# Two fused kernels on one core: one written-out sequence of 1011 operations exchanged for another

## The chip, the cores and the metric

The kernel runs on one core of a Trainium2 chip. The metric is the device time of one execution in microseconds; the value used is the median of several runs. A core has five engines that run side by side, each working through its own instructions strictly in order: TensorE (PE in the profile, its weight loads PEld), VectorE (DVE), ScalarE (ACT), GpSimd (POOL) and SyncE (SP), which here only issues transfers. GpSimd issues transfers too, those that add into their target.

## The reference

The first half is an attention without softmax. With a = S1 x and b = S2 x (8 values each), phi(x) is the outer product of a and b (64 values). The output of this half becomes the input x of a second half that mixes tokens.

```python
q_p, k_p = (phi(q), phi(k))                       # (4, 4, 1088, 64)
kv = np.einsum('bhsf,bhsd->bhfd', k_p, v)
z = np.sum(k_p, axis=2)
num = np.einsum('bhsf,bhfd->bhsd', q_p, kv)
den = np.einsum('bhsf,bhf->bhs', q_p, z)[..., None] + 1e-06
x = num / den                                     # then laid out as (4, 1088, 128)
...
theta = x @ w_theta
zr, zi = x * np.cos(theta), x * np.sin(theta)
y = einsum('ts,bsd->btd', w_tok_r, zr) + einsum('ts,bsd->btd', w_tok_i, zi)
u = x + y
out = u + np.maximum(u @ w_ch, 0.0)
```

There are 4 batches, 4 heads, 1088 tokens and 128 channels. The denominator is small against its terms, so the kernel computes it in several exact slices (the "levels").

## The kernel before

**Operations and sequence.** The kernel does not issue instructions while it walks its loops. Each piece of work is first recorded as an operation (`L.op`, line 133) with an engine, a planned duration, a function that issues its instructions, and the buffers that it writes and reads. 1011 operations are recorded, numbered in the order of recording. The text `ORDER` (line 29) names these numbers in the sequence in which they are issued. `lay` (line 207) walks that sequence once with the planned durations; its start times decide two things alone: which slot of a buffer class each buffer gets (line 229), and how many filler matmuls `issue` (line 273) puts ahead of an operation for which the plan has TensorE wait (line 279). A filler is a 128x384 bf16 matmul on zeros (`spin`, line 434, L435 in the profile); 11 stand at the very start (line 438), 16 more are operations of their own (the "fill" stage, line 440), and one is a marker (line 1432). Because every engine runs in order, the place of a number in `ORDER` fixes what each instruction stands behind on its engine, and on SP and POOL which transfer is issued behind which.

**Stages, as far as the steps below need them.** Names in quotes are those of the tiles in the profile.

- The first transfers (SP): the keys of batch 0 (`load`, line 674), the small matrices S1 and S2 ("st", lines 454 and 455), the two square weights ("zs" from w_sq, `weight` line 646), then keys, queries and values of the other batches and the 17 row blocks of the token-mixing weights (w_tok, 1088 KB each). The weights come as 64-bit floats and are rebuilt as 32-bit floats by ACT (L647, L649) and DVE (L388, L384).
- Key sums (`key_sums`, line 683): ACT squares a batch's keys (L699), a matmul with ones adds them up ("ps<-sm,ones"), DVE derives a rounding step (L388 "sm<-sm") and rounds the keys ("hf<-big,sm"), then takes the remainder ("big<-big,hf"). TensorE sums products of the rounded keys ("ps<-hf", 36 narrow matmuls) and of the remainders ("ps<-big,big" and "ps<-big", the rest sums).
- Key features (`kfeatures`, line 769): TensorE transposes keys (L792), ACT copies them out (L795), TensorE applies S1 and S2 ("ps<-sbk,g"), DVE forms the outer products ("g<-sm,ps"), TensorE multiplies with the values ("ps<-g,big" 128x64).
- `chain` (line 838) and `levels` (line 1050) make the exact denominator: short DVE and TensorE steps, then nine groups of four matmuls for each batch ("ps<-mv,hf" and "ps<-mf,big", 128x96), ACT's copy (L1068), and a chain of DVE steps on "lv".
- `outputs_x` (line 1129): numerators (transposes L1155, "ps<-g,sm"; for batches 2 and 3 `small_numerators`, line 1100, with DVE transposes L1112 and one block of 64 narrow matmuls "ps<-zs,g"), then theta, sine and cosine on ACT (L1197 to L1203). `balance` (line 1218) squares two batches' x on ACT (L1222) and puts a common scale on them, which the third batch's phases wait for.
- Token mixing: "ps<-big,zs" with 128x384 and 128x320 for batches 0 and 1 (`mix_row`, line 1247), and for batches 2 and 3 together a Strassen-Winograd product (`winograd`, line 1299) with half-sized blocks (288 and 256 wide).
- `finish` (line 1273) and `finish_by_tokens` (line 1289): last weight, ReLU and sum on DVE (L391), transpose on DVE (L1279), and the store by SP: four transfers for each block (L1283), one for each of the two last blocks (L1297).

**Matmuls and instructions.** A transpose or a bf16 or f16 matmul is one weight load and one matmul in the trace; another f32 matmul of the program is two such pairs. The program's 1253 matmuls are 2066 in the trace, with as many weight loads.

Of the kernel before, what the change touches and what calls it, by code (L numbers as in the profile page):

```python
# [26 lines left out]
TINY = 2.0**-60  # L27
UP = 256.0
ORDER = """
    0 1 35 12 5 13 10 11 107 14 53 15 16 18 54 108 57 55 101 19 58 20 47 48 59 17 3 4 60 61 62 63 64 65 66 38 67  # L30
    68 21 138 142 125 50 144 36 102 79 95 69 49 70 71 56 72 40 73 74 22 80 81 309 96 311 147 23 51 75 24 126 145
    7 250 257 261 28 127 82 39 97 128 129 251 98 25 8 99 103 310 143 312 104 105 139 76 77 78 140 31 263 192 193
    146 41 307 308 166 84 119 120 32 85 33 37 131 266 313 109 86 148 149 267 132 150 151 110 111 167 168 314 186
    100 344 268 269 152 153 87 88 205 209 345 106 112 154 244 9 347 113 133 187 42 188 134 26 264 89 2 245 34 90
    91 189 43 285 135 198 199 194 195 141 92 93 155 238 156 157 270 271 272 273 158 274 159 160 161 262 162 163
    6 211 164 165 286 287 121 239 29 122 27 114 190 315 123 346 171 348 200 201 94 364 424 116 428 425 426 429
    432 214 233 427 215 216 359 202 430 44 360 169 431 433 434 435 234 235 288 236 252 316 206 333 172 436 117
    366 327 124 437 438 196 45 253 173 207 210 439 328 217 118 174 175 440 317 339 83 441 442 365 325 170 176
    326 443 318 319 320 321 191 130 136 115 444 334 177 331 265 178 445 323 197 453 52 137 240 324 246 446 341
    241 332 30 213 247 179 203 204 180 335 336 454 460 449 322 46 340 450 447 218 219 242 220 221 222 258 275  # L40
    276 342 277 278 279 448 456 455 457 349 394 451 248 458 212 452 280 350 343 351 259 181 467 281 535 536 469
    531 470 537 532 463 459 533 282 283 534 527 528 529 538 461 530 539 223 224 225 226 227 228 254 464 476 183
    540 182 462 229 230 231 468 471 465 352 473 541 472 474 466 184 284 542 232 475 477 478 543 353 354 544 355
    243 545 546 547 548 484 249 255 256 549 356 384 483 492 493 485 185 386 361 479 480 556 481 260 486 494 385
    552 553 550 551 357 559 560 557 558 554 563 561 555 571 562 208 564 565 482 358 362 367 487 374 566 567 578
    570 572 489 289 573 574 575 576 363 488 368 329 579 369 495 290 568 580 569 581 370 371 496 497 375 291 577
    292 582 586 490 641 642 643 491 588 377 583 293 589 372 376 584 618 619 595 585 294 620 295 296 297 644 645
    379 646 380 381 621 590 622 596 623 373 419 330 396 395 592 591 298 498 668 669 670 303 382 421 383 671 672
    673 674 675 378 664 665 420 397 237 300 404 387 666 587 593 409 422 597 388 598 647 648 649 650 411 624 594
    423 406 305 410 405 389 667 398 412 676 599 600 601 602 299 301 391 407 413 408 390 603 604 499 392 393 399  # L50
    400 401 500 414 306 836 402 403 415 677 651 652 678 501 502 416 679 417 503 504 505 506 302 680 418 507 681
    508 515 682 683 840 509 337 684 685 688 690 338 686 687 730 726 727 731 732 728 521 729 865 722 723 724 653
    304 835 654 510 869 733 605 625 839 626 627 628 629 691 725 834 689 692 693 734 735 736 694 695 737 696 655
    630 631 738 739 740 741 742 743 632 698 746 748 697 699 744 747 700 656 701 511 512 705 657 707 703 749 658
    708 709 702 711 745 606 633 713 750 751 704 752 753 516 814 815 715 706 795 796 797 816 710 714 607 513 712
    817 798 755 804 837 754 756 716 717 777 779 780 863 719 799 781 818 819 718 522 868 768 770 800 759 761 720
    771 772 805 762 820 757 782 763 806 774 838 867 841 773 807 808 809 810 811 758 721 760 634 767 769 514 764
    801 893 608 864 765 635 766 831 776 775 778 783 784 832 861 802 851 852 821 853 854 833 891 862 523 524 855
    856 822 857 803 860 880 858 785 525 926 889 881 882 890 859 907 894 866 883 884 885 659 892 636 886 786 929
    930 870 823 827 787 788 789 790 609 895 928 791 792 793 610 908 887 896 794 871 872 873 909 910 932 911 912  # L60
    874 875 876 877 517 518 913 914 888 915 828 931 842 965 933 916 934 843 844 845 927 878 879 948 846 847 949
    950 920 939 848 849 850 812 935 937 813 637 897 638 639 936 526 611 612 613 951 940 924 952 953 954 898 899
    900 901 902 964 938 941 942 943 944 829 640 955 903 956 519 824 520 825 826 977 987 988 925 660 945 946 947
    661 830 662 663 960 904 905 966 989 614 906 615 967 968 969 616 961 617 921 917 918 919 970 971 972 973 957
    974 922 923 975 990 962 978 979 991 958 959 976 997 998 992 980 993 999 994 995 963 1000 996 981 982 983 984
    985 986 1006 1008 1007 1009 1001 1002 1010 1003 1004 1005
"""
WARM = 0
FILL = 5.0
# [36 lines left out]
class Layout:  # L106
# [26 lines left out]
    def op(self, eng, dur, fn, w=(), r=(), hold=(), lk=0, fly=0.0, chan=0.0):  # L133
        o = Op()
        o.lk, o.fly, o.stage, o.chan = lk, fly, self.stage, chan
        o.i, o.eng, o.dur, o.fn = len(self.ops), eng, dur, fn
        pred = set()
        o.bufs = []

        def parts(x):  # L140
            return x if isinstance(x, tuple) else (x, None)

        def hits(table, b, key):
            t = table.get(b, {})
            return [v for k, v in t.items() if k is None or key is None or k == key]

        for x in r:
            b, key = parts(x)
            pred.update(hits(self.last_w, b, key))
            o.bufs.append(b)  # L150
        for x in w:
            b, key = parts(x)
            pred.update(hits(self.last_w, b, key))
            for s in hits(self.readers, b, key):
                pred.update(s)
            o.bufs.append(b)
        for x in r:
            b, key = parts(x)
            self.readers.setdefault(b, {}).setdefault(key, set()).add(o.i)
        for x in w:  # L160
            b, key = parts(x)
            if key is None:
                self.last_w[b] = {None: o.i}
                self.readers[b] = {}
            else:
                self.last_w.setdefault(b, {})[key] = o.i
                self.readers.setdefault(b, {})[key] = set()
        o.bufs = list(dict.fromkeys(o.bufs + list(hold)))
        for b in o.bufs:
            b.ops.append(o.i)  # L170
        pred.discard(o.i)
        o.pred = sorted(pred)
        self.ops.append(o)
        return o
# [145 lines left out]
def kernel(  # L320
# [13 lines left out]
    S, DM = out.shape[1], out.shape[2]  # L334
# [35 lines left out]
    op, buf = L.op, L.buf  # L370
# [78 lines left out]
    sp = fixed((2, NS), F32, "sp")  # L449
# [7 lines left out]
    if wide:  # L457
        st = fixed((NS,), I64, "st")
        y = fixed((NS,), I32, "sy")
        z = fixed((NS,), I32, "sz")  # L460
        op("V", 0.1, lambda: V.memset(st().bitcast(F32), 0.0), [st], [])
        op("S", 0.25, read_small, [st], [], lk=3)

        def words():
            w = st().bitcast(I32).rearrange("p (n t) -> p n t", t=2)
            return w[:, :, 0], w[:, :, 1]

        op("A", 0.25, lambda: A.activation(sp()[:, 0], words()[1].bitcast(F32), AF.Prelu, scale=2.0**-112,
                                           alpha=-(2.0**32)), [(sp, 0)], [st])

        def unpack():
            wl = words()[0]
            x = sp()[:, 0].bitcast(I32)
            ts(x, x, 3, ALU.logical_shift_left)
            stt(x, wl, 29, x, ALU.logical_shift_right, ALU.bitwise_or)
            ts(y(), x, -(1 << 23), ALU.bitwise_and)
            ts(z(), wl, 0x1FFFFFFF, ALU.bitwise_and)

        op("V", 0.85, unpack, [(sp, 0), y, z], [st], lk=2)
        op("A", 0.25, lambda: A.activation(sp()[:, 1], z(), AF.Copy, scale=2.0**-52), [(sp, 1)], [z])  # L480
        vop(NS, lambda: tt(V, sp()[:, 1], sp()[:, 1], y().bitcast(F32), ALU.mult), [(sp, 1)], [y])
    else:
        op("V", 0.2, lambda: V.memset(sp(), 0.0), [sp], [])
        op("S", 0.25, read_small, [(sp, 0)], [], lk=3)

    def powers(mfn, m, n, name):

# [1013 lines left out]
```

## Time and profile before

| what | value |
|---|---|
| median of 3 runs | 222.49 us (221.52 to 222.84) |
| the profiled execution | 222.86 us |
| its span, first to last instruction | 221.1 us, so 1.76 us lie around it |
| PE busy | 212.8 us (96%), 2066 matmuls |
| DVE, ACT, POOL busy | 167.0, 114.9, 45.5 us |
| filler matmuls | 39 |
| bytes moved by transfers | 40.19 MB |

A busy PE means that at least one matmul is in flight; matmuls overlap, so how long one holds the engine is read from the distance between two starts, not from its duration. In a line of the timeline the brackets at its end say how long the engine was idle before and what ended that; "issue" means that nothing the profile shows held the instruction back. A row of the stretches view gives, for each engine, its busy time in that stretch and, behind an x, the number of its instructions.

### The profile page before, as it was taken

To read this page: it belongs to the slowest core of one execution; us is meant where nothing else is said; L and a number is where in the kernel's file an instruction comes from. 1 tells how busy PE (TensorE), PEld (TensorE's weight loads), DVE (VectorE), ACT (ScalarE), POOL (GpSimd) and SP (SyncE) were. 2 spreads that over 40 slices of the span, in tenths; PEclk is the share of its full clock that TensorE was granted. 3 is DMA by queue.
4 is the path that set the end of the run, shared out by engine and by line. 5 is a ranking of instruction groups with operands and counts; after the bars stand their busy time and mean duration, and the time that the engine had idled before them with its cause. 6 is when DMAs were issued, how large, how long until landed. Compare 5 with 4: busy or idle time off the path is not lost.

```text
span 221.1 us, 5129 instructions
## 1 busy us (share of the span) xinstructions
PE 212.8 (96%) x2066; PEld 160.8 (73%) x2066; DVE 167.0 (76%) x360; ACT 114.9 (52%) x237; POOL 45.5 (21%) x81
## 2 busy tenths in 40 slices
PE   7999998999999999999999999999999999999993
PEld 3786987777776757686666685778888787788772
DVE  2899897999899999899999969953899005324951
ACT  3988657989699798949740042377930000000000
POOL 1168260101200000100040083000273165030000
PEclk9999999999999999999999999999999999999999
DMA  6999999985509008948862069411098489772673
GB/s 183 411 424 319 394 418 362 418 270 211 205 9 369 30 0 268 373 170 260 345 115 41 0 104 178 73 20 20 0 185 139 80 149 180 122 111 34 100 115 69
DMA packets 26987, 40.19 MB, mean 182 GB/s; under 512 B 18260, under 2 KB 19284, under 8 KB 24788
## 3 DMA queue, kind: packets, MB, share of 16 engines
q1 hardware_dynamic: 22212, 30.30, 40.0%
q0 software_dynamic: 4752, 9.57, 24.4%
q8 instruction: 16, 0.26, 0.4%
q14 instruction: 7, 0.06, 0.1%
HBM read 28.07 MB, written 2.23 MB: 137 GB/s over the span
## 4 chain that ended last, share of the span: by engine, by line
PE 80%; DVE 5%; ACT 5%; SPq 3%; DMA 3%; issue 2%
PE ps L404 73%; SPq L1283 3%; DMA big<-k_l 2%; PE ps L1188 2%; PE ps L1155 2%; PE ps L792 2%; ACT big L649 2%; PE ps L435 1%; DVE lv L384 1%; DVE g L384 1%; DMA out<-g 1%; PE ps L1035 1%; ACT big L699 1%; DVE big L391 1%; ACT big L1003 1%
## 5 line engine op out<-in xcount | busy, mean ns | idle before, releaser
L404 PE MATMUL ps<-big,zs 128*128 128x384 f32 (+4 forms) x366 | 102.8, 426 | 0.4 <-DVE big L384 0.4
L404 PEld LDWEIGHTS ps<-big,zs 128*128 128x128 f32 x366 | 65.6, 190 | 27.6 <-DVE big L384 1.6
L1267 ACT COPY g<-ps 128x384 f32<-128x384 f32 (+1 forms) x6 | 2.6, 464 | 44.6 <-DVE g L1279 32.0
L384 DVE CUSTOM_DVE_ANT_0 big<-big,big 128x2176 uint16<-128x2176 uint16 x17 | 21.5, 1285 | 0.3
L647 ACT ACTIVATE big<-zs 128x1088 f32<-128x1088 f32 x17 | 20.6, 1215 | 2.3 <-DMA zs<-w_tok 1.8
L649 ACT ACTIVATE big<-zs 128x1088 int32<-128x1088 uint32 (+1 forms) x18 | 20.8, 1167 | 1.1 <-DVE big L384 1.1
L404 PE MATMUL ps<-mf,big 128*128 128x96 f32 x72 | 14.6, 296 | 0.9 <-issue 0.9
L384 DVE TENSOR_TENSOR zs<-ps,g 128x768 f32<-128x768 f32 (+2 forms) x20 | 12.3, 629 | 3.6 <-ACT g L1201 2.2
L391 DVE SCALAR_TENSOR_TENSOR big<-ps,even,big 128x256 f32<-128x256 f32 (+1 forms) x10 | 4.8, 493 | 12.6 <-PE ps L404 12.6
L404 PE MATMUL ps<-big,big 128*32 128x32 f32 (+2 forms) x320 | 14.1, 220 | 0.2 <-issue 0.2
L1328 POOL DMA_DIRECT2D big<-zs x8 | 7.0, 1132 | 34.7 <-PE ps L404 29.4
L1328 POOL DMA_DIRECT2D big<-big x8 | 9.2, 1638 | 19.7 <-issue 19.7
L404 PEld LDWEIGHTS ps<-big,big 128*32 128x32 f32 (+1 forms) x320 | 10.3, 118 | 3.4 <-issue 1.5
L398 POOL DMA_DIRECT2D g<-big x6 | 7.8, 1433 | 23.4 <-ACT g L1267 23.4
L1295 ACT COPY g<-ps 128x128 f32<-128x128 f32 x2 | 0.5, 265 | 23.0 <-PE ps L1293 22.0
L388 DVE TENSOR_SCALAR big<-big 128x1088 int32<-128x1088 int32 x17 | 12.1, 719 | 0.0
L404 PEld LDWEIGHTS <-hf 128*32 128x32 bf16 (+1 forms) x252 | 10.8, 99 | 1.7 <-issue 0.5
L435 PE MATMUL ps<-idle 128*128 128x384 bf16 x39 | 10.6, 398 | 1.3 <-POOL idle L437 1.3
L404 PEld LDWEIGHTS ps<-mf,big 128*128 128x128 f32 x72 | 10.9, 191 | 1.1 <-issue 1.1
L384 DVE TENSOR_TENSOR g<-lv 128x768 f32<-128x768 f32 x12 | 11.1, 953 | 0.3
L404 PE MATMUL ps<-w,big 128*128 128x128 f32 x76 | 10.9, 280 | 0.4 <-ACT g L1295 0.4
L404 PEld LDWEIGHTS ps<-w,big 128*128 128x128 f32 x76 | 9.9, 192 | 1.5 <-ACT g L1295 0.6
(199 smaller groups left out, 399.6 us busy)
## 6 DMA issues: line engine op xcount, KB each, us to landing
zs<-w_tok SPq DMA_DIRECT2D x17, 1088.0 KB, 5.6
big<-k_l SPq DMA_DIRECT2D x7, 576.0 KB, 8.1
big<-q_l SPq DMA_DIRECT2D x4, 576.0 KB, 15.6
big<-v_l SPq DMA_DIRECT2D x4, 576.0 KB, 8.0
big<-big POOLq DMA_DIRECT2D x8, 272.0 KB, 6.1
big<-zs POOLq DMA_DIRECT2D x8, 272.0 KB, 3.9
zs<-big POOLq DMA_DIRECT2D x8, 272.0 KB, 5.7
big<-hf POOLq DMA_DIRECT2D x3, 576.0 KB, 9.9
```

The lines of the kernel that those rows point to most:

```text
L384: eng.tensor_tensor(out=o, in0=a, in1=b, op=f)
L388: (eng or V).tensor_scalar(out=o, in0=a, scalar1=s1, scalar2=s2, op0=op0, **kw)
L391: (eng or V).scalar_tensor_tensor(out=o, in0=a, scalar=s, in1=b, op0=op0, op1=op1)
L398: op("G", 1.05, lambda: G.dma_start(dst(), src(), accum_op=ALU.add), w, r, chan=chan)
L404: T.matmul(o, lhs, rhs, start=start, stop=stop, skip_group_check=True)
L435: T.matmul(nowhere(), idle()[:, 0:P], idle(), start=True, stop=True, skip_group_check=True)
L647: op("A", 0.22 + n * 0.0009, lambda: A.activation(dfn(), words_of(raw(), n)[1].bitcast(F32), AF.Prelu, scale=2.0**-112, alpha=-(2.0**32)), ...
L649: op("A", 0.22 + n * 0.0009, lambda: A.activation(stp(), words_of(raw(), n)[0].bitcast(U32), AF.Copy, scale=2.0**-29), [stp], [raw])
L792: T.transpose(tr()[:, i * P:(i + 1) * P], kx()[:, g * GC + i].rearrange("p h d -> p (h d)"), ident())
L1155: T.transpose(tr()[:, i * P:(i + 1) * P], qp()[:, i * H + 2 * n:i * H + 2 * n + 2].rearrange("p h i j -> p (h i j)"), ident())
L1283: SY.dma_start(out[b, t0 - o:t0 + w, f * SQ:(f + 1) * SQ].rearrange("(c j) i -> j c i", j=SQ), ot()[f * SQ:(f + 1) * SQ, :o + w].rearrange ...
L1328: op("G", 1.05, lambda i=i: G.dma_start(dst[0](i), x[0](i), accum_op=ALU.add), [dst[1](i)], [x[1](i)], chan=ADD_FLY3)
```

## The change

The text `ORDER` is replaced by another sequence of the same 1011 numbers. The planned duration of the transfer of S1 and S2 goes from 0.25 to 0.9 (this is a number of the plan; it changes no instruction). Slots and fillers follow from the new walk.

```diff
 ORDER = """
-    0 1 35 12 5 13 10 11 107 14 53 15 16 18 54 108 57 55 101 19 58 20 47 48 59 17 3 4 60 61 62 63 64 65 66 38 67
-    68 21 138 142 125 50 144 36 102 79 95 69 49 70 71 56 72 40 73 74 22 80 81 309 96 311 147 23 51 75 24 126 145
-    7 250 257 261 28 127 82 39 97 128 129 251 98 25 8 99 103 310 143 312 104 105 139 76 77 78 140 31 263 192 193
...
+    0 1 35 107 12 10 101 11 13 53 57 54 38 14 15 55 58 102 16 3 18 138 47 60 61 62 63 64 65 66 48 67 68 108 19
+    59 17 95 142 56 125 69 70 71 72 73 74 36 79 4 20 50 21 144 22 40 49 51 96 80 81 75 309 147 23 7 24 145 250
+    257 126 261 6 28 97 251 98 99 103 104 127 311 82 39 41 76 148 149 150 151 143 128 105 129 77 139 25 166 78 8
...
-    974 922 923 975 990 962 978 979 991 958 959 976 997 998 992 980 993 999 994 995 963 1000 996 981 982 983 984
-    985 986 1006 1008 1007 1009 1001 1002 1010 1003 1004 1005
+    969 970 971 972 973 974 959 975 976 989 990 991 992 997 979 993 980 981 982 963 994 995 998 999 1000 996 983
+    984 985 986 1006 1008 1007 1001 1002 1009 1010 1003 1004 1005
 """
...
-        op("S", 0.25, read_small, [st], [], lk=3)
+        op("S", 0.9, read_small, [st], [], lk=3)
...
-        op("S", 0.25, read_small, [(sp, 0)], [], lk=3)
+        op("S", 0.9, read_small, [(sp, 0)], [], lk=3)
```

What moves, seen from each engine's own instruction list in the built programs:

- TensorE: 40 fillers in place of 39. At the start 11 run ahead of the first real work (13 before), then six transposes of the first keys (three before), the ones matmul and 8 fillers. The rest of the list is the same instructions in another sequence almost throughout.
- ACT: the squares of the first keys stand ahead of the conversion of S1 and S2 (behind it before). Later, the first of the two squares of `balance` stands ahead of the third batch's first phase step (behind nine of its steps before).
- DVE: the first rounding step stands ahead of the four small steps that rebuild S1 and S2 (behind them before), and these stand between it and the rounding of the keys.
- SP: the second batch's keys are fetched ahead of the square weights (behind before); of the long transfers some change places; of the stores, the second block of batch 0 goes out ahead of the third (behind before).
- POOL: the adding transfers change places among themselves.

## Prediction

> **What bounds the kernel now.** I read the totals first, then the stretches, then who waits for whom, and at last the timeline of the few waits.
>
> ```profile
> PE 212.8 (96%) x2066; PEld 160.8 (73%) x2066; DVE 167.0 (76%) x360; ACT 114.9 (52%) x237; POOL 45.5 (21%) x81
> ...
> PEclk9999999999999999999999999999999999999999
> ```
>
> TensorE is busy for 96% of the span, at the full granted clock. From 50 to 210 us every ten-microsecond stretch has it busy for 10.00 (one has 9.76). Nothing in the change shortens a matmul, so time can come only from what TensorE does besides: wait, or run fillers.
>
> ```profile
> PE ps L404 <- issue: 2.2, 4, 0.9
> PE ps L435 <- POOL idle L437: 1.3, 1, 1.3
> PE ps L404 <- DVE big L384: 0.4, 1, 0.4
> PE ps L404 <- ACT g L1295: 0.4, 1, 0.4
> PE ps L1155 <- ACT g L1159: 0.2, 1, 0.2
> PE ps L1035 <- issue: 0.2, 1, 0.2
> ```
>
> All waits of TensorE: behind the first, at the start, they come to 3.4 us, and 2.4 of them have no releaser ("issue"). These lie here:
>
> ```profile
> 15.20 0.28 PE L404 MATMUL ps<-sm,ones 128*128 128x1 f32 x2 [0.16 <-issue]
> ...
> 22.43 0.25 PE L404 MATMUL ps<-g,big 128*32 128x64 f32 x3 [0.86 <-issue]
> ...
> 28.71 0.23 PE L404 MATMUL ps<-big,big 128*32 128x32 f32 x4 [0.21 <-issue]
> ...
> 35.24 0.35 PE L404 MATMUL ps<-mf,big 128*128 128x96 f32 x1 [0.94 <-issue]
> ```
>
> Three of the four are in the middle of a group whose inputs were there. Cutting the span at these points, and at the last such wait (47.82), shows why:
>
> ```profile
> 15.19:22.42 7.23, 6.37 (x126) 4.95 (x125) 6.85 (x19) 6.13 (x19) 5.98 (x19) 1.00 1.02 344
> 22.42:28.70 6.28, 6.07 (x125) 5.57 (x126) 5.28 (x16) 3.73 (x11) 1.28 (x3) 1.00 1.02 396
> 28.70:35.23 6.53, 5.58 (x128) 4.94 (x127) 6.13 (x18) 4.62 (x11) 3.71 (x9) 1.00 1.03 407
> 35.23:47.81 12.58, 12.34 (x253) 10.44 (x253) 10.97 (x29) 11.32 (x29) 0.86 (x1) 1.00 1.03 377
> ```
>
> TensorE's matmuls and weight loads between two waits are 251, 251, 255 and 506, which is 256, 256, 256 and 512 with the few semaphore instructions. The transfer queues say the same:
>
> ```profile
> q8 instruction: 16, 0.26, 0.4%
> ```
>
> Sixteen packets, so 16 KB each; the transfer view cut into small stretches has one at 12.8 to 13.9, 20.1 to 21.1, 26.2 to 27.3, 32.7 to 33.9, 38.9 to 39.9 and 45.3 to 46.3, and each wait ends 1.3 to 1.5 us behind one. I read these packets as TensorE's instructions, 256 at a time, fetched when the block ahead is begun, and late because the last column's 344 to 407 GB/s keep the transfer engines full (DMA share 1.02). Counted in instructions, blocks begin at B1 9.43, B2 15.20, B3 22.43, B4 28.71, B5 35.24, B6 42.39 and B7 47.82. From the begin of a block to the arrival of the next: 5.8, 7.2, 6.3, 6.5, 6.0 (B5's packet ends 39.9, plus 1.4; TensorE came at 42.39 and did not wait) and 5.4. Up to 48 us these are a floor under TensorE, whatever the sequence; the sequence decides how much work lies in each block.
>
> **The start.** 13 fillers at 0.320 before the first transposes become 11: -0.64, so transposes can start at 4.83 (5.47). The first keys allow it: ACT waited until 5.00 only for S1 and S2, and the keys were asked for first. But the six transposes (0.213 each there, still slow) and eight fillers (0.33, then 0.163) fill the time to 8.05, where the first "ps<-hf" matmul stood before. Its input moves: the squares now start at about 4.7 instead of 5.15 (before, they stood behind the wait of S1 and S2), but the four small DVE steps (5.28 to 6.02, 0.74) now stand between the rounding step and the rounding: 7.68 - 0.45 + 0.74 = 7.98, and the remainder, 9.14 before, comes at 9.35. The rest sums waited for it (0.08 of slack), so B1 goes from 9.43 to 9.64: +0.2. Bounds: 0 (keys land early) and +0.5 (at 5.0). The fetch of the second batch's keys ahead of the square weights (one 0.35 issue, 256 KB) lets ACT begin their squares at about 7.5 (7.85 before); TensorE reaches them no sooner, so I count nothing; the weights' conversion then comes 1.6 later, off the path, since its matmuls run at 52.
>
> **The blocks.** Each block of the new list is summed as count times the distance between two starts in the trace, switches included (narrow 128x64 products 0.020, "ps<-sbk,g" 0.112, transposes 0.11 to 0.15, a pair of fillers 0.33 to 0.45, one level group 0.39).
> - B1 to B2: 5.9 (before 5.9), plus 0.1 because the scaling matrix, behind the later DVE steps, is ready at 10.9. B2 = 15.6.
> - B2 to B3: 6.1, eight fillers among it. The fetch needs 7.2, and what made it long, the first w_tok block's transfer (issued at 6.93, twelfth in both), is still there. B3 = 22.8. Bounds 21.7 (work alone) and 22.9.
> - B3 to B4: 72 narrow products 1.41, 18 "sbk" passes 2.02, 9 transposes 1.31, six fillers 1.41, the rest 1.34: 7.5, above the fetch's 6.3. B4 = 30.3.
> - B4 to B5: 6.54, fetch 6.5, with eight of nine level groups (3.1) now in this block. B5 = 36.85.
> - B5 to B6: 5.3, fetch 6.0. B6 = 42.9.
> - B6 to B7: 5.0, fetch 5.4. B7 = 48.3.
>
> So B7 is 0.5 later. Less is done by then: without fillers, 34.35 us of work against 34.68, 0.33 short. Together +0.8. The fillers themselves cost nothing more: two slow ones out, three fast ones in.
>
> **The middle.** The last level group ends 0.4 behind B5, at 37.2 (37.3 before), and the DVE steps behind it are the same 8.6 us, so the first numerator transposes find their input at the same time, and TensorE arrives for them at 48.4. Elsewhere I compared, for each matmul, how far it moved in TensorE's list with how far its DVE or ACT producer moved in its own: all but a handful keep some tenths. The tightest is the third DVE transpose ("zs<-g", ready 144.80 for TensorE's block at 145.09): one DVE step of 0.72 now stands ahead of it, and the first phase step of the third batch, on which DVE waits, stands behind ACT's square of 1.18. It is ready at about 146.0; TensorE comes at 145.9 plus the 0.8. I count nothing; bounds 0 and 0.5. POOL's adding transfers keep at least 6 us to their readers, against 4 to 7 from issue to landing: nothing.
>
> **The end.** The store of batch 0's third block now starts at about 201.3 with another behind it. From 202.48 to 217.34 SP issued 28 stores, 0.53 each; 32 now take 17.0, to 218.3. The last two stores need SP at 217.9 and 218.6: even, so nothing; bounds 0 and +0.5. The last matmuls, ACT copy and DVE step are the same.
>
> **Sum.** The profiled execution took 222.86 (span 221.1 and 1.76 around it); +0.8 is 223.66. It stood 0.37 above the median, 222.49, so I forecast 223.3. Within 1% (2.2 us) a measurement of this kernel hardly tells a change from none.
>
> [...]
>
> **Rivals.**
> - *The fetch does not bind* (its packets come sooner because the long transfers change places). Then the blocks cost their work alone: B7 = 9.64 + 0.1 + 36.3 = 46.0, 1.8 earlier, less the 0.33: -1.5, so 221.0. For it: nothing ties the delays of 3.4 to 4.9 us from the begin of a block to the packet to this sequence. Against it: five blocks in a row show them, and the bytes are the same.
> - *More goes away.* All waits behind the start (2.7 up to 71 us) and 0.1 of fillers gone: 219.7, a floor. It needs the fetch and every producer early at once.
> - *The middle binds, slower.* In ACT's list the square of 1.18 stands ahead of the third batch's first phase step, and the scaled copy of x, which waits for DVE, ahead of the last phase step. If that third DVE transpose ends later than TensorE's arrival at about 146.7, each further microsecond is one of time: up to 1.2 there and 0.8 at the scaled copy, 225.3. For it: slacks of 0.1 to 0.5 in this stretch. Against it: ACT is idle for 2.5 us just ahead (138.3 to 140.85), which is where the square goes.
> - *The slow clock lasts longer.* Distances fall from 0.320 to 0.163 only at about 6.8, behind one filler and three transposes. If six transposes in place of fillers put that off past the eight fillers, these cost 1.26 more and B1 comes 1.0 later: 224.3. [...]
>
> **Chances.** Forecast 0.55, the fetch not binding 0.18, more 0.06, the middle 0.15, the slow clock 0.06. The range from 220.9 to 225.4 leaves out the floor case and the far end of the middle. The forecast's own range, from its bounds, is 222.2 to 224.6. Faster by over 1% is the floor case, 0.06; slower by over 1% most of the middle, 0.14; within 1%, 0.80.
>
> **What would show it.** Right: waits of "issue" every 256 instructions at about 15.6, 22.8, 42.9 and 48.3, the largest at 22.8 (1.1), none at 30.3; the first rest sums about 0.2 later; TensorE busy throughout from 50 to 210. Wrong: block ends without waits, a wait of TensorE on DVE or ACT of more than 0.5 between 138 and 162, or SP issuing the last stores late.

## The result, and the profile after

The changed kernel takes 225.18 us (median of six executions, 223.19 to 226.04), the kernel before 222.38 in the same session (220.96 to 222.84): a ratio of 1.0126, 95% interval 1.0096 to 1.0156. The change costs 2.8 us. The time lies in the range forecast, near its upper end, and 1.9 above the number forecast. That it lies in the range is luck in part: the forecast's own bounds, 222.2 to 224.6, do not hold it, the range does only because a rival whose mechanism did not occur stretched it to 225.4, and "slower by over 1%" had been given 0.14. The profiled execution took 226.04, with a span of 224.2. Ratios leave out single executions more than 1.5% above the fastest; counts of executions below hold them all.

The totals of the page, and the row of TensorE's granted clock over 40 slices:

```profile
PE 214.8 (96%) x2067; PEld 161.9 (72%) x2067; DVE 166.6 (74%) x360; ACT 116.3 (52%) x237; POOL 46.3 (21%) x81
...
PEclk9999999988999999999999999999999999999999
```

The reader is to see the two eights: before, the row held nines only. TensorE is as busy as it was, 96%, but part of its busy time runs on a slower clock. The stretches view shows where (after the time: busy microseconds and count of PE, PEld, DVE, ACT, POOL; then the granted clock, the DMA share and GB/s):

```profile
46.00:47.00 1.00, 0.56 (x5) 0.43 (x5) 1.00 (x2) 0.34 (x1) 0.00 (x0) 1.00 1.01 313
47.00:48.00 1.00, 0.28 (x3) 0.19 (x2) 1.00 (x3) 0.00 (x0) 0.00 (x0) 1.00 1.06 388
48.00:49.00 1.00, 0.54 (x5) 0.42 (x4) 0.99 (x3) 0.79 (x2) 0.00 (x0) 1.00 1.00 406
49.00:50.00 1.00, 1.00 (x10) 0.83 (x9) 0.84 (x6) 0.76 (x2) 0.00 (x0) 0.61 0.46 182
50.00:51.00 1.00, 1.00 (x6) 1.00 (x5) 0.86 (x6) 1.00 (x4) 0.53 (x2) 0.50 0.08 35
51.00:52.00 1.00, 1.00 (x6) 0.68 (x4) 1.00 (x2) 0.80 (x2) 0.02 (x1) 0.50 0.00 0
52.00:53.00 1.00, 1.00 (x5) 0.30 (x4) 1.00 (x2) 0.48 (x1) 0.00 (x0) 0.68 0.00 0
```

Three microseconds in which TensorE has little to do are followed by some three in which it is always busy and at half the clock. The trace's clock record gives 49.22 to 52.63, which is 3.41 us; half of that, 1.7 us of work, is lost. What emptied the time ahead are two waits, in the timeline of TensorE:

```profile
47.72 0.27 PE L1035 MATMUL ps<-ident,big 128*128 128x128 f32 x1 [1.16 <-issue]
47.84 0.36 PE L404 MATMUL ps<-sm,ones 128*128 128x4 f32 x2
48.66 0.33 PE L1155 MATMUL ps<-ident,g 128*128 128x128 f32 x1 [0.46 <-ACT big L1038]
```

The same place before:

```profile
47.29 0.33 PE L1035 MATMUL ps<-ident,big 128*128 128x128 f32 x1
47.82 0.44 PE L1035 MATMUL ps<-ident,big 128*128 128x128 f32 x2 [0.20 <-issue]
48.10 1.41 PE L1155 MATMUL ps<-ident,g 128*128 128x128 f32 x9
```

The first wait is the fetch of block B7, whose packet landed at 46.28, 1.44 ahead of the wait's end. It cuts the last group of query transposes (L1035) in two, so that only its third transpose lies behind the wait. ACT can copy the group out only then (L1038), and the first numerator transposes (L1155) have been given the bank of just this group ("ps" slot 2 in the walk of `lay`): they wait for the copy. Before, the group had slot 6 and the first three groups of numerator transposes slots 2, 7 and 4. All waits of TensorE of 0.3 and more (the one of L792 is the fetch of B3, at 21.93):

```profile
PE ps L1035 <- issue: 1.4, 2, 1.2
PE ps L435 <- POOL idle L437: 1.3, 1, 1.3
PE ps L1155 <- ACT big L1038: 0.5, 1, 0.5
PE ps L792 <- PE ps L404: 0.4, 1, 0.4
PE ps L404 <- DVE big L384: 0.4, 1, 0.4
PE ps L404 <- ACT g L1295: 0.4, 1, 0.4
PE ps L404 <- ACT big L807: 0.3, 1, 0.3
PE ps L404 <- ACT big L1003: 0.3, 1, 0.3
```

**Where the 3.2 us between the two profiled executions (222.86 and 226.04) went.** The eighth of the nine groups of the last batch's levels starts at 129.69 before and at 132.18 after: +2.49, of which +0.70 are waits of TensorE, 1.7 the half clock, and 0.1 the rest. From there to the last matmul it is 87.77 and 88.06: +0.29, of which about 0.2 is a wait of the last batch's transposes on ACT's scaled copy of x, seen in the weight loads (L1188, 0.28 empty behind ACT's L1180 at 160.27; of the matmuls' own time only 0.09 is empty there). From the last matmul to the end it is 3.61 and 3.99: +0.38. There the queue of SP is what is late. The kernel before, then after (start, time, line, transfers):

```profile
202.48 14.86 SPq L1283 DMA_DIRECT2D out<-g  x28
217.76 1.02 SPq L1297 DMA_DIRECT2D out<-g  x2
```

```profile
203.92 17.07 SPq L1283 DMA_DIRECT2D out<-g  x32
221.09 0.87 SPq L1297 DMA_DIRECT2D out<-g  x2
```

Before, the queue is free at 217.34 and the two last stores start as their data come, 0.30 us behind the start of the last matmul (217.46). After, four more stores keep it until 220.99; the first of the two last had its data at 220.51 and starts at 221.09, 0.85 behind the last matmul (220.24), and the second must wait for it.

### The profile page after: what moved, and what is told of

It reads as the page before. It is cut to its first block, busy times and chain, and to the rows that moved or that the text cites. A ratio compares the mean times of both kernels' runs of the same rounds, so it can differ in the third digit from the quotient of the medians.

```text
span 224.2 us, 5126 instructions
## 1 busy us (share of the span) xinstructions
PE 214.8 (96%) x2067; PEld 161.9 (72%) x2067; DVE 166.6 (74%) x360; ACT 116.3 (52%) x237; POOL 46.3 (21%) x81
## 4 chain that ended last, share of the span: by engine, by line
PE 83%; ACT 6%; DMA 4%; DVE 2%; SPq 1%; issue 1%
PE ps L404 74%; DMA big<-q_l 3%; PE ps L1155 3%; PE ps L1188 2%; PE ps L435 2%; PE ps L1035 1%; PE ps L792 1%; ACT big L1038 1%; SPq L1283 1%; DVE g L391 1%; DMA out<-g 1%; DVE zs L384 1%; ACT big L1126 1%; ACT big L1003 1%; ACT big L649 1%
## 5 line engine op out<-in xcount | busy, mean ns | idle before, releaser
L398 POOL DMA_DIRECT2D g<-big x6 | 8.9, 1748 | 31.1 <-ACT g L1267 31.1
L404 PE MATMUL ps<-big,big 128*32 128x32 f32 (+2 forms) x320 | 13.6, 220 | 0.1
L1328 POOL DMA_DIRECT2D big<-zs x8 | 7.9, 1109 | 25.6 <-PE ps L404 23.4
```

The source lines that it names most:

```text
L398: op("G", 1.05, lambda: G.dma_start(dst(), src(), accum_op=ALU.add), w, r, chan=chan)
L404: T.matmul(o, lhs, rhs, start=start, stop=stop, skip_group_check=True)
L1328: op("G", 1.05, lambda i=i: G.dma_start(dst[0](i), x[0](i), accum_op=ALU.add), [dst[1](i)], [x[1](i)], chan=ADD_FLY3)
```

## The experiments

The first theory: the two waits ahead of 48.7 lose the clock, and that, with 0.8 us in the head (up to 48 us), is the loss. The rivals: the drop has nothing to do with the waits; or the loss lies in the new rest of the sequence.

In what follows an execution counts as having lost the clock where its mean granted clock is 0.992 or less: one step of 3.41 us at half clock takes 1.7 of some 222 us, which is 0.008.

**Two instructions fewer, at the same time.**

```diff
-    first = op("P", 3.6, lambda: [spin() for _ in range(11)], [nowhere], [idle])
+    first = op("P", 3.6, lambda: [spin(n) for n in 7 * [GW] + 3 * [512]], [nowhere], [idle])
```

> The changed kernel with its first 11 fillers of 384 columns written as 7 of 384 and 3 of 512: 10 fillers, the same 4224 columns and so the same time, but two instructions fewer. By my count of instructions the third 'ps<-ident,big' transpose of the last query group, which was the first one behind the fetch wait at 47.72 us, then falls into the block ahead of that wait. Theory (the two waits close together, 1.16 on the fetch and 0.46 on ACT's copy of that transpose, make the clock drop to half from 49.2 to 52.6): the wait on ACT is gone, about 1.0 to 1.1 us of fetch wait stays, the granted clock stays at 1.00 between 49 and 53 in the profile, and the median comes to 223.2 to 223.9 (the changed kernel's one execution with a mean clock of 1.000 took 223.19). If the fetch wait alone is enough for the drop: no wait on ACT, but the clock at 0.50 as before, 224.7. Rival (the drop has nothing to do with these waits, or the loss lies elsewhere in the sequence): 225.2 +- 0.5, mean clock 0.990 to 0.997.

Measured: 224.82, ratio 1.0120 (1.0083 to 1.0156). In its profile all three transposes stand ahead of the block's end, and the wait on the copy is gone:

```profile
46.66 0.50 PE L1035 MATMUL ps<-ident,big 128*128 128x128 f32 x3
48.09 0.39 PE L404 MATMUL ps<-sm,ones 128*128 128x4 f32 x2 [0.94 <-ACT big L807]
48.33 0.52 PE L1155 MATMUL ps<-ident,g 128*128 128x128 f32 x3
```

(The releaser named there, ACT's copy from 47.67 to 47.98, is not what the matmul needs: in the changed kernel it ran at 47.84, ahead of that copy at 48.50. The packet of the block landed at 46.70, 1.39 ahead of the end of the wait.) So the block ends behind the same number of matmuls, 852, as in the changed kernel, and the count of 256 holds. The clock stays at 1.00 in the profile, but two of six executions have a mean clock of 0.992 or less, and the others are at 224.4 in the middle: a miss by some 0.5, and no gain over the changed kernel's executions that kept their clock. The fetch then ends 0.4 later, and takes up what the other wait gave back.

**Work put into the wait.** The fillers are also made wider, as in the next experiment; of the edit only what that one does not have is shown.

```diff
             def trs(g=g, tr=tr):
+                for _ in range(8 if b == 3 and g == 0 else 0):
+                    T.matmul(tr(), idle()[:, 0:P], idle()[:, 0:GW], start=True, stop=True, skip_group_check=True)
```

> The changed kernel with the same filler columns in fewer and wider instructions (512 columns in place of 384; 16 instructions fewer by 47 us), and with 8 fillers of 384 columns more (16 instructions, 1.3 us) ahead of the next to last group of query transposes, in the block that ends in the fetch wait of 47.72. The block's end so lies at the same transpose as in the changed kernel. Theory: TensorE works through most of the wait; 1.16 us of waiting becomes 0 to 0.4, the wait of 0.46 on ACT may stay, the clock stays at 1.00, and the median is 223.2 to 223.6, 1.6 to 2.0 less with 1.3 us of work more. Rival (the clock's drop is unrelated): 225.2 to 226.5, clock 0.99.

Measured: 224.13, ratio 1.0105 (1.0070 to 1.0140); mean clock 0.997 or more in all six executions. In the timeline the block's end costs nothing now, the wait on ACT stays, and the clock is 1.00 throughout (this file's lines stand four lower):

```profile
44.79 1.47 PE L1037 MATMUL ps<-idle 128*128 128x384 bf16 x8
...
48.21 0.55 PE L1159 MATMUL ps<-ident,g 128*128 128x128 f32 x3 [0.53 <-ACT big L1042]
```

With 1.3 us more of useless work the kernel is no slower than the changed one: its median is 1.0 to 1.5 lower than the two medians measured for that (the intervals of the ratios overlap), and no execution lost the clock, where seven of twelve did. That agrees with what the theory says of the drop, but does not show it: the next experiment has the wider fillers alone, without the work in the wait, and kept its clock too. Beside that one, which takes 223.22, the 1.3 us of work cost 0.9. The time is 0.5 above what the theory gave.

**The same filler columns in fewer instructions.**

```diff
-        op("P", 0.335, lambda: [spin() for _ in range(2)], [], [idle], hold=[nowhere])
+        op("P", 0.335, lambda i=i: [spin(512) for _ in range(1 + i % 2)], [], [idle], hold=[nowhere])
```

> The changed kernel with the same filler columns in fewer and wider instructions (512 columns in place of 384), nothing else: 16 instructions fewer by 47 us. Theory (up to 48 us the arrival of each block of 256 instructions sets the pace): the blocks begin when they did, to 0.5 us, but each ends 4 to 16 instructions later in the list, so that 0.4 to 0.6 us more work is done by the last of these waits; the wait on ACT at 48.66 is gone, since its transpose lies ahead of the block's end. With the clock kept: 222.6 to 222.9; with the clock still halved for 3.4 us: 224.5. Rival (the sequence's own work sets the pace, the fetch only takes up slack): 225.2, or 223.2 where the clock is kept.

Measured: 223.22, ratio 1.0059 (1.0035 to 1.0083), the clock kept in all twelve executions. That is 0.9 below the 224.14 of the changed kernel's executions with their clock kept (five in two other sessions, 223.19 to 225.42); 0.4 to 0.6 was expected of the instructions. It is what one would see if the arrival of the instructions sets the pace in this sequence. The wait on ACT is still there (0.57 at 46.85), against the expectation, with another of 0.60 on DVE at 48.59; the clock survives these 1.16 us of waiting, all in one step of its record.

**The new head with the old rest.**

In the file the list is written out; in short:

```diff
+ORDER = new[:300] + [i for i in old if i not in new[:300]]
```

> The new sequence up to the last group of query transposes (the one that the fetch wait of 47.72 cuts), and then the remaining operations as the kernel before has them in relative order. The head's instructions, slots and fillers are those of the changed kernel; in the rest the first numerator transposes get other slots, none of them that of the last query group. Theory: the fetch wait of about 1.2 at 47.7 stays, the wait on ACT goes, and the clock is kept: 223.0 to 223.4 (the head's forecast 0.8 more than before). If the fetch wait alone halves the clock: 224.7. Rival (the new rest, from 48 us on, carries a loss of its own): 222.4 to 222.6, with the clock at 1.00.

Measured: 222.97, ratio 1.0039 (1.0012 to 1.0066), one of twelve executions with a lost clock. The head costs 0.3 to 1.5 us, as forecast. (The fetch wait of about 1.2 at 47.7, which was expected to stay, is 0.46 at 48.14 in this profile, with one of 0.97 at B3; so the run does not tell whether the longer wait alone keeps the clock.) So the other 1.9 us of the loss need the new rest, and that includes the meeting of head and rest at 48 us, where the old rest gives other banks.

**The changed kernel again.** No edit.

> The changed kernel itself, run again beside the other three. So far an execution's time follows its mean granted clock c: time less 222 us x (1 - c) is 223.2 to 224.1 for its six executions. Theory (its two waits before 49 us lose the clock in some executions): again about half of the executions with c at 0.992 or lower, these 1.5 to 2 us slower than those at 1.000, and a median of 224.5 to 225.3. Rival (the drops were chance): c at 0.996 or more in all but one, as in 23 executions of the kernel before, and a median of 223.6.

Measured: 225.65, ratio 1.0146 (1.0092 to 1.0200). Four of six executions with a mean clock of 0.992 or less. Over both sessions, the seven of twelve that lost it are at 225.88 (median), the five others at 224.14: 1.74 apart, the 1.7 of one halved step. Both profiled executions are among those that lost it, in the step that holds the two waits. The kernel before lost it in 4 of 62 executions; its others are at 221.78.

**A wait put into the kernel before.**

```diff
+            if o.i == 454:
+                fill(self.ops[335].bufs[1])
...
-            op("A", act(GW) + 0.1, lambda g=g, tr=tr: A.activation(f()[:, g * GW:(g + 1) * GW], tr(), AF.Copy,
-                                                            scale=s()[:, 0:1]), [(f, g)], [tr, (s, 0)])
+            op("A", act(GW) + 0.1, lambda g=g, tr=tr: [A.activation(f()[:, g * GW:(g + 1) * GW], tr(), AF.Copy,
+                                                            scale=s()[:, 0:1])
+                                                      for _ in range(3 if b == 3 and g == 2 else 1)], [(f, g)], [tr, (s, 0)])
```

> The kernel before with one wait put in where the changed kernel has its second: ACT's copy of the last group of query transposes (L1038, 0.58 us) is done three times instead of once, and one filler (0.16 us) ahead of the first numerator transposes writes into the bank that it reads, so that TensorE must wait for it. By the trace of before the wait runs from about 48.2 to 50.0, behind a fetch wait of 0.2. Theory (idle time of TensorE of 1.6 us or more within some 3 us loses the clock): the clock falls to 0.50 for about 3.4 us soon behind it, in most executions, and the time is 1.2 to 2.0 for the wait and 1.7 for the clock above before: 224.9 to 225.7, mean clock 0.99. Rival (the drop has another cause): the clock stays, and only the wait is lost: 223.2 to 224.0.

Measured: 225.52, ratio 1.0157 (1.0107 to 1.0207). All six executions lost the clock, four of them by their mean clock (0.985 or less) for more than one step. The wait in the timeline and the stretches around it:

```profile
48.84 0.46 PE L437 MATMUL ps<-idle 128*128 128x384 bf16 x1 [1.90 <-ACT big L1040]
```

```profile
47.00:48.00 1.00, 0.00 (x0) 0.00 (x0) 0.90 (x5) 0.97 (x2) 0.00 (x0) 1.00 0.98 321
48.00:49.00 1.00, 0.16 (x1) 0.16 (x1) 0.86 (x6) 0.97 (x3) 0.18 (x1) 0.94 0.66 258
49.00:50.00 1.00, 1.00 (x6) 0.92 (x6) 0.93 (x4) 0.88 (x1) 0.36 (x2) 0.50 0.29 114
```

This decides between theory and rival: a wait alone, in the kernel that hardly ever loses its clock, loses it, and the price fits the wait (1.9) and one halved step (1.7): 221.78 and 3.6 is 225.4.

**The old head with the new rest.**

```diff
+ORDER = old[:307] + [i for i in new if i not in old[:307]]
```

> The reverse of the exchanged halves: the sequence of before up to the last group of query transposes, with its fillers and slots, and then the remaining operations in the new relative order. Theory (three losses: about 1.0 in the new head up to 48 us, 0.5 to 0.9 in the new rest, most of it at the very end, and the clock only where head and rest meet): 222.5 to 222.9, ratio 1.003 to 1.005, mean clock 0.998 or more, TensorE's last matmul 3.9 us before the end (3.6 in before). Rival (the new rest loses nothing): 222.0. Rival (the clock is lost by the new rest): 223.5 or more with clocks of 0.992.

Measured: 226.49, ratio 1.0167 (1.0103 to 1.0230), three of six executions with a lost clock. The theory and the first rival missed; the second rival fits the time, but not the profiled execution, which took 224.57 with its clock kept. Where the halves meet, this kernel has waits that neither of the two has, 0.54 and 1.56, both on DVE, so it says nothing on the new rest by itself. It says something else: the wait of 1.56 did not lose the clock in its profile.

```profile
49.00:50.00 1.00, 0.00 (x0) 0.00 (x0) 0.96 (x3) 0.28 (x1) 0.20 (x1) 1.00 0.15 61
50.00:51.00 1.00, 0.73 (x6) 0.64 (x6) 1.00 (x2) 0.18 (x1) 0.00 (x0) 1.00 0.00 0
51.00:52.00 1.00, 1.00 (x11) 0.33 (x9) 1.00 (x2) 0.73 (x3) 0.00 (x0) 1.00 0.06 16
```

**The old tail.**

```diff
+ORDER = new[:725] + [i for i in old if i not in new[:725]]
```

> The new sequence up to the operation that starts at 151.4 in its trace (148.8 in before's), and from there the remaining operations in the relative order of before. Theory (the new order of the last stores makes SP late by 0.3 us, and a split of the last batch's phase matmuls costs 0.2): the last matmul stands 3.6 us before the end instead of 3.96, and from that operation to the last matmul it is 68.67 instead of 68.87; the median is 0.5 below that of the changed kernel run beside it. Rival (the end is even, as forecast): the same median as the changed kernel's.

Measured: 225.07, ratio 1.0142 (1.0089 to 1.0195), against 225.65 of the changed kernel beside it; four of six executions lost the clock, as there. The intervals overlap, so the times alone do not show the 0.5; the traces do. From the eighth group of the last batch's levels to the end it is 91.4 us, as in before (91.4), where the changed kernel has 92.1 and 91.9 in its two profiles. The wait on the scaled copy is gone with it, and SP again has 28 stores ahead of the last two, which start 0.30 behind the last matmul:

```profile
205.08 14.97 SPq L1282 DMA_DIRECT2D out<-g  x28
220.37 1.02 SPq L1296 DMA_DIRECT2D out<-g  x2
```

**A shorter wait in the kernel before.** As above, with two copies in place of three (`range(2 if ...)`).

> The kernel before with the same added wait as in the run with three copies, but with two copies instead of three: a wait of about 1.3 us where that one was 1.90. Theory (the granted clock is set anew in steps of 3.41 us, and falls to half for one step when TensorE was idle for more than about 1.57 us of the step before, since 1.58 to 1.62 and 1.90 lost it and 1.56 did not): few executions with a mean clock of 0.992 or lower, at most 2 of 6, only where a fetch wait lies in the same step; 1.3 for the wait, so about 223.0. Rival (any wait that long costs the clock): 0.992 or lower in most executions, 224.7.

Measured: 223.93, ratio 1.0095 (1.0061 to 1.0129). Four of eleven executions lost the clock; in the profile a wait of 1.28 did not:

```profile
48.00:49.00 1.00, 0.00 (x0) 0.00 (x0) 0.91 (x4) 0.97 (x2) 0.00 (x0) 1.00 0.64 245
49.00:50.00 1.00, 0.76 (x7) 0.73 (x7) 0.85 (x5) 1.00 (x2) 0.16 (x1) 1.00 0.21 83
```

The share of lost clocks is near the bound expected, and far from "most"; the executions that kept it are at 223.86, 2.1 above before's 221.78 for a wait of 1.3, which I can't account for in full.

**Fewer filler instructions in the kernel before.** The first edit is the one of the wide fillers above; the second makes each of the eight filler operations one filler of 512; the third empties them (`lambda: None`).

> The kernel before with the same filler columns in fewer instructions (512 columns in place of 384): 14 instructions fewer by 47 us, the same filler time. Theory (up to 48 us a block of 256 instructions takes some 6.2 us to arrive, 24 ns for each instruction): 0.3 us less, ratio 0.998 to 0.999, no mean clock under 0.993. Rival (the fetch does not bind): the same time.

> The same, and the eight filler operations of the list (16 fillers of 384 columns, 3.1 us of TensorE) as eight fillers of 512 (1.7 us): 22 instructions fewer by 47 us, and 1.4 us less filler work. Theory: the missing filler work turns into waits on the fetch, and only the 22 instructions gain: 0.5 less than before, ratio 0.9975. Rival (the fillers cost their time): 1.4 less, 0.994.

> The kernel before with those eight operations empty: 32 instructions and 3.1 us of fillers fewer. Theory: 0.8 less from the instructions, 2.3 us more of waiting spread over 15 to 40 us; where more than 1.57 us of it falls into one step of 3.41 the clock is lost once, 1.7 us, so the median lies between 0.8 less (no loss) and 0.9 more. Rival (the fillers cost their time): 3.1 less, 218.6, ratio 0.986.

Measured: 223.39 (1.0042, 1.0003 to 1.0080), 222.82 (1.0030, 0.9996 to 1.0063) and 229.88. None gained, and the three theories missed, the third by far: at most 0.9 more was expected, and its profile has six steps at half clock. The clock was lost in 4 of 12, 3 of 12 and 5 of 6 executions; those that kept it in the first two are at 222.60 and 222.07, not below 221.78. So the fillers neither cost their time, as the rival had it, nor do fewer instructions gain in this sequence as they did in the new one; why not is open (in before the fetch is not what every block waits for). And the fillers are what keeps the clock: without the eight operations one execution in six kept it. No version here beats the kernel before.

## Why the prediction was right and wrong, point by point

- **"Nothing in the change shortens a matmul, so time can come only from what TensorE does besides."** This is the step that failed. It holds only while the clock is full, which I took for given from a row of nines. The change lengthened matmuls: one step of 3.41 us at half the clock, 1.7 us, in 7 of 12 executions. None of my rivals had it; the one on the clock looked at the start, where the clock came no later than before (full from 4.84, against 6.78; the 8 fillers at 6.09 are fast, 1.46 together).
- **The start** was forecast 0.2 later. The rounded keys came at 7.67 (7.98 forecast) and the rest sums at 9.06 (9.35), so B1 lies at 9.27 instead of 9.64: keys and DVE steps were a little faster, nothing of weight.
- **The blocks.** Forecast B2 to B7: 15.6, 22.8, 30.3, 36.85, 42.9, 48.3. Measured: 15.63, 21.93, 28.99, 35.73, 41.24, 47.72. The waits at B2, B3 and B7, and none at B4, came as forecast; the one at B6 did not come, and the largest (1.16) was at B7, not at B3 (0.41). The second profile of the changed kernel, in the run of it again, is nearer to the forecast: no wait at B2, but 0.85 for B3 at 22.36, 0.68 for B6 at 42.56 and 1.12 for B7 at 48.89. Its waits:

```profile
PE ps L1035 <- issue: 1.1, 1, 1.1
PE ps L792 <- DVE big L384: 0.9, 1, 0.9
PE ps L404 <- issue: 0.7, 1, 0.7
```

(The DVE step named at L792 had ended at 21.73, and the packet of the block landed at 20.89.) The step that was off is the size of the fetch counted from the begin of a block. From B6 it took 6.5 and 6.3 where I took 5.4, from B2 6.3 where I took 7.2. The packet for B7 starts 4.1 and 4.0 behind the begin of B6 in the two profiles of the changed kernel, and 3.0 in that of before; that a block is asked for when the one ahead is begun was my reading of these times, and neither that nor what sets the delay among the long transfers is shown by a run here.
- **The head in all, +0.8.** The size held as a time: the new head with the old rest stands 0.9 above before, ratio 1.0039 (1.0012 to 1.0066). Its working, B7 0.5 later, did not hold in each execution: B7 begins at 47.72, 48.14 and 48.89 in the three profiles with the new head, against 47.82. In the first pair of profiled executions the loss does not show; that of before was 1.1 above the middle of its kernel (222.86 against 221.78).
- **Waits behind the head: none forecast.** The 0.46 on L1155 was missed. I compared how far matmuls and their producers moved; this wait is on a bank, and which bank an operation gets changes with the sequence. The prediction did not follow the banks.
- **The middle, +0 (0 to 0.5).** Nearly right: the third DVE transpose made TensorE wait for nothing; the scaled copy of x, named in the third rival, is late by 0.2.
- **The end: "even, so nothing", 0 to +0.5.** Wrong within its bounds: 0.38 of SP. The prediction's own numbers said so: with 32 stores up to 218.3, the first of the last two, due at 217.9, starts 0.4 late, and the second, half a microsecond behind it, starts at 218.8 instead of 218.6. "SP issuing the last stores late" was one of its signs of being wrong, and it came.
- **The rivals.** The fetch not binding (221.0) and the floor (219.7): no. The middle (225.3) gives nearly the time measured, for a reason that did not occur; the sign that I named for it, a wait of more than 0.5 between 138 and 162, is absent. The fetch does bind in this stretch: three of six block ends have waits, 0.25, 0.41 and 1.16. That a packet is late because the transfer engines are full was too simple: in before's profile the share of the transfer engines is 1.09 from 130 to 140 and 1.04 from 180 to 190 as well, without a wait; there the packets of instructions lie up to 28 us apart (146.90, 173.12, 200.96).

The sum as the runs have it, an estimate from the medians of executions that keep their clock, several sessions together (221.78 to 224.14, +2.4): about 1.1 for the head, 0.5 for the bank, 0.6 to 0.7 for what lies behind the last batch's levels (the scaled copy and SP), and 0.1 to 0.2 not assigned; and 1.7 more whenever the clock is lost.

## What to carry to other kernels

In these runs a wait cost its own length and then, beyond a point, half of the next clock step (1.7 us, in four profiles behind 1.58 to 1.90 of idle time in one step): look at how much idle time falls together, not only at the sum, before calling a reordering free. A new sequence moves buffers as well as instructions, so the waits to look for include those on a slot that an operation has newly inherited. And a row of full clock in one profile is one execution: the mean clock of the others tells how near the edge it is.

## What the runs showed of the hardware that was not expected

**The clock changes on a grid of its own.** The clock record changes only at multiples of 3.413 us from each other: in before's profile the full clock holds for 215.04, which is 63 steps; in the changed kernel's first profile it holds for 44.37, then half for 3.41, then full for 170.67, which is 13, 1 and 50 steps. By the stretches view the half clock lasts from 50.34 to 53.76 in the changed kernel's second profile, from 48.88 to 52.30 in before with a wait put in, and from 27.56 to 37.80 in before with wide fillers: one, one and three steps, to 0.02. And the grid lies differently in each execution: the clock first becomes full at 6.78 in before's profile, at 4.84 and 5.97 in the two of the changed kernel. The waits of 47.72 and 48.66 lie within 2.1 us, so a step can hold both in some executions and split them in others. That would give the same kernel its two sets of times, 1.74 apart; the two profiles both have a step that holds both, and no execution that kept its clock was profiled. Here 1.16 and 0.46 of waiting in one step lost the clock, and so did a single gap of 1.90.

**Idle time alone does not sort the steps.** Idle sums of 1.58, 1.59, 1.62 and 1.90 in a step lost the clock (the changed kernel's second profile, the old tail, the changed kernel's first, and the wait of three copies), and so did 1.68 and, just behind the start, 1.53 in before without its eight filler operations. But 1.56 kept it (the old head with the new rest), and in the profile of before with wide fillers a step with 0.43, but made of transposes and matmuls with few columns, lost it. An estimate from the traces that sorts better: add up, for each step, the columns that each matmul streams times the share of the array's 128 columns that it uses (a "128*32" counts a quarter), with transposes double (at full clock their starts lie 0.109 us apart, where 128 columns would take 0.054), as time at full clock (0.424 ns for a column, from the 0.163 us between two fast fillers of 384), placed at the matmul's end. The steps that lost the clock have 0.55 to 0.90 us of 3.41 (the two profiles of the changed kernel 0.79 and 0.78), but for one just behind the start with 1.14; the one with the wait of 1.56 has 1.19; of 843 that kept it two lie below 0.9 (0.58 and 0.89); and the lowest in before's profile is 0.99. So before too is near the edge where narrow matmuls stand (0.99, 1.09 and 1.02 in the steps from 20.44, 27.26 and 34.09), and the fillers hold it above: without the eight operations five of six executions lost the clock. The border was fitted to these profiles afterwards, on seven steps that lost, and it is not sharp: placed at the matmuls' starts, the step of the wide fillers comes to 1.00 and the lowest of before to 0.92. Transposes do seem to count, from one step: in the changed kernel with wide fillers the step from 45.75 to 49.16 has 1.16 of waits and hardly any columns but those of transposes (0.04 us without them), and kept the clock. No run here varied the border by itself, so its form stays open.
